# A fused attention and ELU feed-forward kernel: token blocks of 512, 512, 512 and 256 in place of four batches of 448

## The chip, the core and the metric

The kernel runs on one core of one Trainium2 chip. The metric is the device time of one execution in microseconds. Three runs of the kernel before gave 648.57, 648.53 and 648.56 us; their median is 648.56 us.

## What is computed

The reference is attention with a soft cap on the scores, followed by two dense layers with an ELU between them. All of it is float32.

```python
batch, n_heads, seq, head_dim = (4, 12, 448, 64)      # attention
n_tokens, d_model, d_ff = (1792, 768, 2048)           # layers

scores = (1 / sqrt(head_dim)) * (q @ k.T)
scores = cap * tanh(scores / cap)                     # cap = 30
attn = softmax(scores)
x = (attn @ v)  -> rows of 768 = 12 heads * 64        # 1792 tokens
h = x @ w_in
g = where(h > 0, h, exp(min(h, 0)) - 1)
out = g @ w_out
```

## The kernel before

**Numbers as pairs.** The layers' products are float32 products made of three passes. Each operand is split into a higher part and a lower part that TensorE takes in one pass each (type fp32r): `xh`, `xl` for the tokens, `wh`, `wl` for the weights, `gh`, `gl` for what comes out of the ELU. A product is `wh*xh + wh*xl + wl*xh`, three matmuls that add up in one PSUM bank. A matmul here is a pair of instructions: the weights (128 by 128) are loaded (PEld in the profile), then the columns of tokens are streamed (PE).

**Attention.** Twelve rounds, each for two of the 24 pairs of heads. The order of the work in a round is written out as a table of times (`AT`), sorted once, and each engine gets its instructions in that order. ACT does tanh and exp of the scores. VectorE (DVE) splits q and k, adds and normalises, splits the first weights, and from round 5 on also splits x of the first batch (`split`, lines 172 and 180). The table `END` orders the end of the attention, where the first hidden units start: both hidden tiles of batch 0, then the splits of batch 1.

**Layers.** `d_ff` is worked off in 8 rounds r of two hidden tiles i (FT = 2, 256 hidden channels), and in each round over the 4 batches b of 448 tokens. A unit (r, b) has a first half, `first` (lines 228 to 240): for each of two tiles, 6 channel tiles by 3 matmuls give h in PSUM, then the ELU (`elu`, lines 205 to 221) as a chain over two engines:

- ACT exp of h (line 210), DVE min and add (211), DVE max and add, reading h (214), ACT copy to `gh` (219), DVE subtract to `gl` (220).

The two hidden tiles of a unit have one PSUM bank each (`pv0`, `pv1`), so the next unit's first matmul into `pv0` waits until line 214 of the last one has read it. The second half, `second` (lines 242 to 260), gives 768 output channels as three tiles of two banks (3 buffers), which DVE adds to an accumulator in SBUF (line 268); in round 0 ACT copies instead. In the last round the accumulator is written to DRAM.

**Order.** `Moe.run` (line 273) is software pipelined by one unit: first half of unit i, three steps of a weight, second half of unit i-1, two steps of a weight. Every engine works through its own queue in that order, so an instruction that waits holds up all behind it on its engine.

**Weights.** The next round's four weight tiles come as raw 64-bit pairs and are made on the spot, in five steps (`Weights.steps`): (1) three DVE instructions, lines 107 to 109; (2) ACT, line 119; (3) DVE, line 123, then a GpSimd (POOL) add, line 126; (4) ACT copy to `wh`, line 133, which needs the POOL add; (5) DVE subtract to `wl`, line 137, which needs `wh`. With five steps a unit, each unit makes one weight, and the second half's three DVE adds stand between step 3 and step 5.

Of the kernel before, what the change touches and what calls it, by code (L numbers as in the profile page):

```python
# [7 lines left out]
F32 = mybir.dt.float32  # L8
# [9 lines left out]
P = 128  # L18
BANK = 512
# [13 lines left out]
TINY = 2.0**-15  # L33

# [30 lines left out]
class Weights:  # L65
# [4 lines left out]
    def __init__(self, nc, pool, rawp, pre, w):  # L70
        self.nc, self.pool, self.rawp, self.pre, self.w = nc, pool, rawp, pre, w
        self.late = self.now = None
        self.raw, self.split = {}, {}
        self.nraw = self.nmid = 0

    def buffer(self, k, n, width, dtype):

        if self.late and k % 2:
            tag, bufs = {"wr": ("raw", 2), "wv": ("vf", 3), "wq": ("vf", 3)}[n]
            return self.rawp.tile([P, width], dtype, name=f"{n}{k}", tag=tag, bufs=bufs)  # L80
# [3 lines left out]
        return self.pre[:, at : at + width].bitcast(dtype)  # L84

# [66 lines left out]
class Tokens:  # L152
# [6 lines left out]
    def new(self, p):  # L159
        self.x[p] = self.pool.tile([P, S], F32, name=f"x{p}", tag="x", bufs=NPAIR + 2)  # L160
        return self.x[p]

    def split(self, p):
        self.high(p)
        self.low(p)

    def high(self, p, vector=False):
        x = self.x[p]
        pool, n = (self.early, 2 * PPB) if p < 2 * PPB else (self.late, 2 * PPB)
        xh = pool.tile([P, S], F32R, name=f"xh{p}", tag="xh", bufs=n)  # L170
        if vector:
            self.nc.vector.tensor_copy(out=xh, in_=x)
        else:
            self.nc.scalar.activation(out=xh, in_=x, func=AF.Copy)
        self.parts[p] = (xh,)

    def low(self, p):
        xh = self.parts[p][0]
        xl = self.pool.tile([P, S], F32R, name=f"xl{p}", tag="x", bufs=NPAIR + 2)
        self.nc.vector.tensor_tensor(out=xl, in0=self.x.pop(p), in1=xh.bitcast(F32), op=ALU.subtract)  # L180
        self.parts[p] = (xh, xl)


class Moe:
# [15 lines left out]
    def hidden(self, r, b, i, h):  # L200
        f = r * FT + i
        for c in range(NC):
            self.products(h, self.wt.get(f, 0), c, self.x.parts[b * PPB + c], c == 0, c == NC - 1)

    def elu(self, r, b, i, h):
        nc, sb = self.nc, self.early
        f = r * FT + i
        n = f"{f}_{b}"
        ev = sb.tile([P, S], F32, name=f"e{n}", tag="ev", bufs=2)
# [7 lines left out]
        gh = sb.tile([P, S], F32R, name=f"gh{n}", tag="gh", bufs=4)  # L217
        gl = sb.tile([P, S], F32R, name=f"gl{n}", tag="gl", bufs=4)
        nc.scalar.activation(out=gh, in_=ev, func=AF.Copy)  # L219
        nc.vector.tensor_tensor(out=gl, in0=ev, in1=gh.bitcast(F32), op=ALU.subtract)  # L220
        self.g[f, b] = (gh, gl)

    def begin(self):

        t = self.ps.tile([P, 2, BANK], F32, name="h0", tag="s", bufs=3)
        return [t[:, i, :S] for i in range(FT)]

    def first(self, r, b, behind=()):

        behind = list(behind)  # L230
        for i in range(FT):
            t = self.ps.tile([P, BANK], F32, name=f"h{r * FT + i}_{b}", tag=f"pv{i}", bufs=1)
            h = t[:, :S]
            self.hidden(r, b, i, h)
            if i == 0:
                self.elu(r, b, i, h)
            for p in behind[i * 3 : i * 3 + 3]:
                self.x.split(p)
            if i:
                self.elu(r, b, i, h)  # L240

    def second(self, r, b):
        nc = self.nc
        for e in range(0, NC, 2):
            if (r, b, e) == (NR - 1, B - 1, NC - 2):
                continue
            t = self.ps.tile([P, 2, BANK], F32, name=f"o{r}_{b}_{e}", tag="s", bufs=3)
            for k in range(2):
                self.outputs(t[:, k, :S], r, b, e + k)
            if r == 0:  # L250
                o = self.late.tile([P, 2, S], F32, name=f"acc{b}_{e}", tag="acc", bufs=B * NC // 2)
                self.acc[b, e] = o
                nc.scalar.activation(out=o, in_=t[:, :, :S], func=AF.Copy)
            else:
                self.finish(r, b, e, 2, t[:, :, :S], self.acc[b, e])
        if (r, b) == (NR - 1, B - 1):
            for k in range(2):
                t = self.ps.tile([P, 1, BANK], F32, name=f"last{k}", tag=f"pv{k}", bufs=1)
                self.outputs(t[:, 0, :S], r, b, NC - 2 + k)
                self.finish(r, b, NC - 2 + k, 1, t[:, :, :S], self.acc[b, NC - 2][:, k : k + 1])  # L260

    def outputs(self, acc, r, b, e):
        for i in range(FT):
            f = r * FT + i
            self.products(acc, self.wt.get(f, 1), e, self.g[f, b], i == 0, i == FT - 1)

    def finish(self, r, b, e, n, t, o):
        self.nc.vector.tensor_tensor(out=o, in0=t, in1=o, op=ALU.add)  # L268
        if r == NR - 1:
            out = self.out[e * P : (e + n) * P, b * S : (b + 1) * S]  # L270
            self.nc.sync.dma_start(out=out.rearrange("(e p) s -> p e s", p=P), in_=o)

    def run(self):

        units = [(r, b) for r in range(NR) for b in range(B)]
        for i in range(1, len(units) + 1):
            if i < len(units):
                self.first(*units[i], range((i + 1) * PPB, min((i + 2) * PPB, NPAIR)))
            self.wt.run(WSTEPS - 2)
            self.second(*units[i - 1])  # L280
            self.wt.run(2)
            self.wt.load()


class Attention:
# [158 lines left out]
    def run(self, weights, moe, raw, rawv):  # L444
# [14 lines left out]
        for n in range(rounds):  # L459
# [55 lines left out]
def general_attention(nc, sb, ps, x, con, src, rawp):  # L515
# [62 lines left out]
def attention_elu_kernel(tc, qk, v, cap, w, out):  # L578
    nc = tc.nc
    src = (qk, v)  # L580
    with ExitStack() as outer:
        cp, rawp, xp, wp, early = (
            outer.enter_context(tc.tile_pool(name=n, bufs=1)) for n in ("con", "raw", "x", "w", "early")
# [6 lines left out]
        raw1 = cp.tile([P, QK], F32, name="raw1")  # L590
# [7 lines left out]
        def path(general):  # L598
            tag = "gf"[not general]
            with ExitStack() as ctx:  # L600
                if not general:
                    ctx.enter_context(tc.manual_schedule())
                weights = Weights(nc, wp, rawp, pre, w)
                x = Tokens(nc, xp, early)
                moe = Moe(nc, early, ps, weights, x, out)
                with tc.tile_pool(name=f"at{tag}", bufs=1) as sb, tc.tile_pool(
                    name=f"dr{tag}", bufs=1, space=DRAM
                ) as dr:
                    if general:
                        general_attention(nc, sb, ps, x, con, src, rawp)  # L610
# [3 lines left out]
                        for p in range(2 * PPB):  # L614
                            x.split(p)
# [3 lines left out]
                    else:  # L619
                        Attention(nc, sb, ps, dr, x, con, src, rawp).run(weights, moe, (raw0, raw1), rawv0)  # L620
# [54 lines left out]
```

## Time and profile before

| | before |
|---|---|
| median of three runs | 648.56 us |
| span of the profiled execution, first to last instruction | 646.2 us |
| the profiled execution in all: the profile gives no time outside its span; the median of the runs lies 2.3 us above the span | 648.6 us, if the part around the span is that of the runs |
| PE busy (records) | 633.9 us, 98% |
| weight loads (PEld) busy | 501.8 us, 78% |
| DVE busy | 462.5 us, 72% |
| ACT busy | 296.8 us, 46% |
| POOL busy | 61.4 us, 10% |
| attention, to the first matmul of the layers | 0 to 171.1 us |
| layers, to the last matmul | 171.1 to 640.7 us |

A span is counted from the first to the last instruction of the program. Ends of matmuls are modelled, so for TensorE the times from one start to the next tell more than the durations. The profile's granted TensorE clock is a share of 2.4 GHz.

### The profile page before, as it was taken

The numbers are of one execution on the slowest core, as the hardware profiler recorded it, in microseconds if no ns is written. First come the engines' busy times: TensorE is split into PE (matmuls) and PEld (weight loads), VectorE is DVE, ScalarE is ACT, GpSimd is POOL, SyncE is SP. The second block draws the span as 40 slices with busy tenths as digits, with TensorE's granted clock in tenths as the row PEclk, the third lists the DMA queues.
The fourth block names the chain that finished last, engine by engine and source line by source line (L and its number), as shares of the span: only waits on it lengthen the run. The fifth ranks groups of instructions, "written<-read, shape, count | busy, mean of one in ns | idle before, by whom it ended". The sixth has DMA issues, their size and how long they took to land.

```text
span 646.2 us, 8747 instructions
## 1 busy us (share of the span) xinstructions
PE 633.9 (98%) x3408; PEld 501.8 (78%) x3408; DVE 462.5 (72%) x672; ACT 296.8 (46%) x384; POOL 61.4 (10%) x40
## 2 busy tenths in 40 slices
PE   6999999999999999999999999999999999999996
PEld 3334434343499999999999999999999999999996
DVE  4789999999667656666677776666677776666443
ACT  6999999999816552222322222222222222222110
POOL 0010100110001121111111211111111111111000
PEclk9999999999999999999999999999999999999999
DMA  4455455543143022020202022020202022000224
GB/s 162 140 161 188 135 185 149 169 143 115 37 134 115 1 97 98 2 98 1 99 0 98 10 89 85 13 98 1 97 1 99 6 94 75 24 1 0 86 87 174
DMA packets 30064, 54.38 MB, mean 84 GB/s; under 512 B 13376, under 2 KB 19776, under 8 KB 30016
## 3 DMA queue, kind: packets, MB, share of 16 engines
q1 hardware_dynamic: 30016, 53.75, 24.8%
q8 instruction: 29, 0.48, 0.3%
q14 instruction: 19, 0.16, 0.1%
HBM read 47.97 MB, written 5.59 MB: 83 GB/s over the span
## 4 chain that ended last, share of the span: by engine, by line
PE 86%; DVE 9%; DMA 2%; issue 1%; SPq 0%; POOL 0%; DVEq 0%
PE h L196 12%; PE h L198 12%; PE h L197 12%; PE o L198 12%; PE o L197 12%; PE o L196 12%; PE pv L370 7%; PE s L328 5%; DVE u L392 3%; DVE qkl L323 2%; PE sum L401 2%; DVE num L407 1%; PE s L345 1%; DMA pre<-in_qk_dram 1%; DVE qkh L320 1%
## 5 line engine op out<-in xcount | busy, mean ns | idle before, releaser
L196 PE MATMUL h<-xh,wh 128*128 128x448 f32 x384 | 140.4, 366 | 0.0
L197 PE MATMUL h<-xl,wh 128*128 128x448 f32 x384 | 140.2, 365 | 0.0
L198 PE MATMUL h<-xh,wl 128*128 128x448 f32 x384 | 140.2, 365 | 0.0
L196 PE MATMUL o<-gh,wh 128*128 128x448 f32 x380 | 138.8, 365 | 0.0
L197 PE MATMUL o<-gl,wh 128*128 128x448 f32 x380 | 138.8, 365 | 0.0
L198 PE MATMUL o<-gh,wl 128*128 128x448 f32 x380 | 138.8, 365 | 0.0
L268 DVE TENSOR_TENSOR acc<-o,acc 128x896 f32<-128x896 f32 x83 | 85.8, 1082 | 9.4 <-PE o L198 9.4
L210 ACT ACTIVATE e<-h 128x448 f32<-128x448 f32 x64 | 34.8, 544 | 111.8 <-PE h L198 111.7
L363 ACT ACTIVATE p<-s,cap 128x896 f32<-128x896 f32 x84 | 84.8, 1009 | 2.7
L211 DVE TENSOR_SCALAR e<-e 128x448 f32<-128x448 f32 x64 | 25.1, 392 | 84.8 <-ACT e L210 84.8
L361 ACT ACTIVATE s<-s,tsc 128x896 f32<-128x896 f32 x84 | 81.9, 975 | 4.2 <-PE s L345 2.9
L370 PE MATMUL pv<-p,vf 128*64 128x448 f32 x368 | 79.3, 552 | 1.8 <-DVE num L407 1.7
L196 PEld LDWEIGHTS h<-xh,wh 128*128 128x128 f32 x384 | 72.1, 188 | 7.1 <-issue 1.4
L198 PEld LDWEIGHTS h<-xh,wl 128*128 128x128 f32 x384 | 72.1, 188 | 5.7
L197 PEld LDWEIGHTS h<-xl,wh 128*128 128x128 f32 x384 | 72.1, 188 | 5.7
L196 PEld LDWEIGHTS o<-gh,wh 128*128 128x128 f32 x380 | 71.4, 188 | 5.6
L197 PEld LDWEIGHTS o<-gl,wh 128*128 128x128 f32 x380 | 71.4, 188 | 5.6
L198 PEld LDWEIGHTS o<-gh,wl 128*128 128x128 f32 x380 | 71.4, 188 | 5.6
L219 ACT ACTIVATE gh<-e 128x448 fp32r<-128x448 f32 x64 | 37.0, 578 | 81.4 <-DVE e L214 81.4
L220 DVE TENSOR_TENSOR gl<-e,gh 128x448 fp32r<-128x448 f32 x64 | 40.0, 625 | 41.3 <-ACT gh L219 41.3
L126 POOL TENSOR_TENSOR pre<-pre,wq 128x768 int32<-128x768 int32 x18 | 34.8, 1935 | 349.0 <-DVE pre L123 349.0
L370 PEld LDWEIGHTS pv<-p,vf 128*64 128x64 f32 x368 | 22.3, 136 | 42.9 <-issue 32.0
(70 smaller groups left out, 635.8 us busy)
## 6 DMA issues: line engine op xcount, KB each, us to landing
pre<-in_w_dram SPq DMA_DIRECT2D x18, 768.0 KB, 4.2
wr<-in_w_dram SPq DMA_DIRECT2D x14, 768.0 KB, 5.6
raw<-in_qk_dram SPq DMA_DIRECT2D x22, 448.0 KB, 4.8
vf<-in_v_dram SPq DMA_DIRECT2D x23, 256.0 KB, 4.2
rb<-rec SPq DMA_DIRECT2D x48, 112.0 KB, 2.8
out_dram<-acc SPq DMA_DIRECT2D x11, 448.0 KB, 2.5
den<-sums SPq DMA_DIRECT2D x96, 1.8 KB, 2.3
out_dram<-acc SPq DMA_DIRECT2D x2, 224.0 KB, 3.2
```

The costliest lines, as they stand in the source:

```text
L126: nc.gpsimd.tensor_tensor(out=vi, in0=vi, in1=q, op=ALU.add)
L196: mm(acc, wh[:, m, :], ph, start=first, stop=False)
L197: mm(acc, wh[:, m, :], pl, start=False, stop=False)
L198: mm(acc, wl[:, m, :], ph, start=False, stop=last)
L210: nc.scalar.activation(out=ev, in_=h, func=AF.Exp)
L219: nc.scalar.activation(out=gh, in_=ev, func=AF.Copy)
L220: nc.vector.tensor_tensor(out=gl, in0=ev, in1=gh.bitcast(F32), op=ALU.subtract)
L268: self.nc.vector.tensor_tensor(out=o, in0=t, in1=o, op=ALU.add)
L328: yield lambda a=a, b=b, i=i: self.nc.tensor.matmul(s, a[o, k], b[o, :S], start=i == 0, stop=i == 2)
L361: self.nc.scalar.activation(out=s, in_=s, func=AF.Tanh, scale=self.con.tsc[:, 0:1])
L363: self.nc.scalar.activation(out=pt, in_=s, func=AF.Exp, scale=self.con.cap[:, 0:1])
L370: self.nc.tensor.matmul(out[o, :S], w[j], x[j], **flags)
```

## The change

The 1792 tokens are cut into blocks of 512, 512, 512 and 256 (`BLOCKS`), whatever the batch. A full bank of 512 columns is streamed per matmul in the first three blocks. The block of 256 holds higher and lower part side by side in one tile of 512 columns (`both`), so that `wh` takes both in one matmul of 512 columns, and `wl` takes the higher part alone in one of 256: two matmuls in place of three. Its two halves of h and of the output lie in the two halves of the bank and are added afterwards (`elu_last`, and a second add in `finish`). The split of x is done in pieces where a block crosses two batches. Weight steps go by block: 7, 7, 6 and none. The buffers of odd weights and the first loads also move to other pools. The line numbers of the changed kernel are others: line 254 to 264 there are lines 210 to 220 before, 340 is 268, 124 to 154 are 107 to 137.

```diff
+HALF = BANK // 2
+BLOCKS = [(t, min(BANK, B * S - t)) for t in range(0, B * S, BANK)]
+WRUN = (7, 7, 6, 0)
...
     def products(self, acc, w, m, part, first, last):
-        (wh, wl), (ph, pl) = w, part
-        mm(acc, wh[:, m, :], ph, start=first, stop=False)
-        mm(acc, wh[:, m, :], pl, start=False, stop=False)
-        mm(acc, wl[:, m, :], ph, start=False, stop=last)
+        (wh, wl), (ph, pl, both) = w, part
+        wh, wl = wh[:, m, :], wl[:, m, :]
+        if both is None:
+            mm(acc, wh, ph, start=first, stop=False)
+            mm(acc, wh, pl, start=False, stop=False)
+            mm(acc, wl, ph, start=False, stop=last)
+            return
+        if first:
+            mm(acc, wh, both, start=True, stop=False)
+        mm(acc[:, :HALF], wl, ph, start=False, stop=False)
+        if not first:
+            mm(acc, wh, both, start=False, stop=last)
...
+    def elu_last(self, r, t, hs):
+        two = self.ev(f"s{r}_{t}").rearrange("p (i n) -> p i n", i=FT)
+        for i, h in enumerate(hs):
+            self.nc.scalar.activation(out=two[:, i], in_=h[:, HALF:], func=AF.Copy)
+            self.nc.vector.tensor_tensor(out=two[:, i], in0=h[:, :HALF], in1=two[:, i], op=ALU.add)
+        ev = self.ev(f"{r}_{t}").rearrange("p (i n) -> p i n", i=FT)
+        self.shape(ev, two)
...
+            self.divide(ev[:, i], g[:, 0], g[:, 1])
...
+    def finish(self, r, t, e, n, s, o):
+        if r == 0:
+            self.nc.scalar.activation(out=o, in_=s[:, :, :width], func=AF.Copy)
+        else:
+            self.nc.vector.tensor_tensor(out=o, in0=s[:, :, :width], in1=o, op=ALU.add)
+        if width == HALF:
+            self.nc.vector.tensor_tensor(out=o, in0=s[:, :, HALF:], in1=o, op=ALU.add)
...
-            self.wt.run(WSTEPS - 2)
-            self.second(*units[i - 1])
-            self.wt.run(2)
-            self.wt.load()
+            n = WRUN[units[i - 1][1]]
+            self.wt.run(n // 2)
+            self.second(*units[i - 1])
+            self.wt.run(n - n // 2)
+            self.wt.ahead()
...
-                if 0 <= c < PPB:
-                    at(g + AT["split"][k], *((self.x.high, c, True) if k == 0 else (self.x.low, c)))
-        for c in range(PPB):
-            at(end + END["xh"], self.x.high, PPB + c)
-            at(end + END["xl"], self.x.low, PPB + c)
+                for p in ([c] if 0 <= c < PPB else []) + [PPB + i for i in range(PPB) if n == 8 + i // 2]:
+                    at(g + AT["split"][k], *((self.x.high, p, 0, True) if k == 0 else (self.x.low, p, 0)))
+        for b in (1, 2):
+            for c in range(PPB):
+                at(end + END["xh"], self.x.high, b * PPB + c, 1)
+                at(end + END["xl"], self.x.low, b * PPB + c, 1)
```

Three places show how the queues move. The first is TensorE's queue at the start of a unit's hidden tile (h; `xh`, `xl` or `xb` are the tokens, `wh` and `wl` the weights). Before, any batch:

```order
L196 MATMUL h_1_2058<-xh_1947,wh_522 128x448
L197 MATMUL h_1_2058<-xl_2012,wh_522 128x448
L198 MATMUL h_1_2058<-xh_1947,wl_523 128x448
L196 MATMUL h_1_2058<-xh_1949,wh_522 128x448
L197 MATMUL h_1_2058<-xl_2014,wh_522 128x448
L198 MATMUL h_1_2058<-xh_1949,wl_523 128x448
```

With the change, the block of 256 tokens:

```order
L234 MATMUL h_3_2367<-xb_2260,wh_518 128x512
L235 MATMUL h_3_2367<-xb_2260,wl_519 128x256
L235 MATMUL h_3_2367<-xb_2263,wl_519 128x256
L237 MATMUL h_3_2367<-xb_2263,wh_518 128x512
L235 MATMUL h_3_2367<-xb_2266,wl_519 128x256
L237 MATMUL h_3_2367<-xb_2266,wh_518 128x512
```

Three matmuls of 448 columns per channel tile became one of 512 and one of 256; in the other three blocks there are three of 512.

The second is DVE's queue around a unit's outputs (`acc`), with the weight steps (`pre`, `wv`, `wl`) and the ELU (`e`, `gl`). Before, in every unit:

```order
L123 SCALAR_TENSOR_TENSOR wv_2716<-wr_2552,wv_2716 128x768
L268 TENSOR_TENSOR acc_0_2292<-o_1_0_2724,acc_0_2292 128x896
L268 TENSOR_TENSOR acc_2_2307<-o_1_2_2738,acc_2_2307 128x896
L268 TENSOR_TENSOR acc_4_2322<-o_1_4_2752,acc_4_2322 128x896
L137 TENSOR_TENSOR wl_2767<-wv_2716,wh_2766 128x768
L211 TENSOR_SCALAR e_3_2791<-e_3_2791 128x448
```

With the change, from the middle of round 1 to the first ELU of round 2 (the block of 256 is `es_3`, `e_3`, `g_3`):

```order
L140 SCALAR_TENSOR_TENSOR pre<-pre 128x768
L279 TENSOR_TENSOR es_3_2813<-h_3_2787,es_3_2813 128x256
L279 TENSOR_TENSOR es_3_2813<-h_3_2800,es_3_2813 128x256
...
L154 TENSOR_TENSOR wl_2784<-pre,wh_2783 128x768
...
L340 TENSOR_TENSOR acc_4_2458<-o_2_4_2863,acc_4_2458 128x1024
L140 SCALAR_TENSOR_TENSOR wv_2829<-wr_2672,wv_2829 128x768
L154 TENSOR_TENSOR wl_2880<-wv_2829,wh_2879 128x768
L255 TENSOR_SCALAR e_0_2904<-e_0_2904 128x512
L258 SCALAR_TENSOR_TENSOR e_0_2904<-h_0_2885,e_0_2904 128x512
```

Step 3 (line 140) and step 5 (line 154) of a weight now stand next to each other, ahead of the next ELU; before, three output adds lay between them.

The third is DVE's queue in attention round 9. Before:

```order
L407 COPY num_1524<-pv_1_1472 128x448
L172 CAST xh_1528<-x_875 128x448
L320 CAST qkh_1547<-raw_1450 128x832
L323 TENSOR_TENSOR qkl_1548<-raw_1450,qkh_1547 128x832
L410 COPY sums_1562<-sum_1_1519 128x448
```

With the change:

```order
L486 COPY num_1524<-pv_1_1470 128x448
L200 CAST xh_4_1528<-x_871 128x448
L200 CAST xh_2_1207<-x_1185 128x64
L200 CAST xh_3_1366<-x_1187 128x64
L399 CAST qkh_1549<-raw_1448 128x832
```

Two small casts came in, for the 64 tokens of the second batch that belong to the first block; two small subtracts follow later in the round, and the same in rounds 8 and 10.

## Rows read from the trace of the kernel before

**Rows 1.** The page: busy tenths in 40 slices of the span, and the granted clock.

```profile
PE   6999999999999999999999999999999999999996
DVE  4789999999667656666677776666677776666443
PEclk9999999999999999999999999999999999999999
```

**Rows 2.** Busy time by stretch: PE, PEld, DVE, ACT, POOL, then PEclk, DMA share, GB/s.

```profile
92.00:157.00 65.00, 63.89 (x436) 26.26 (x436) 62.69 (x96) 63.03 (x67) 4.45 (x2) 1.00 0.51 152
330.00:388.00 58.00, 58.00 (x288) 53.76 (x287) 40.15 (x56) 15.58 (x24) 7.42 (x4) 1.00 0.15 55
```

**Rows 3.** Timeline in the layers, TensorE: start us, us, engine, line, out<-in.

```profile
300.00 0.19 PEld L198 LDWEIGHTS h<-xh,wl 128*128 128x128 f32 x1
300.20 0.36 PE L198 MATMUL h<-xh,wl 128*128 128x448 f32 x1
300.20 0.19 PEld L196 LDWEIGHTS h<-xh,wh 128*128 128x128 f32 x1
300.40 0.36 PE L196 MATMUL h<-xh,wh 128*128 128x448 f32 x1
```

**Rows 4.** Timeline of POOL, one add per unit, 20 rows from first to last.

```profile
311.62 1.85 POOL L126 TENSOR_TENSOR pre<-pre,wq 128x768 int32<-128x768 int32 x1 [12.73 <-DVE pre L123]
...
588.89 1.85 POOL L126 TENSOR_TENSOR wv<-wv,wq 128x768 int32<-128x768 int32 x1 [12.75 <-DVE wv L123]
```

**Rows 5.** Timeline of the weight loads in attention, four rows from first to last.

```profile
150.40 0.14 PEld L370 LDWEIGHTS pv<-p,vf 128*64 128x64 f32 x2 [0.23 <-issue]
...
151.52 0.14 PEld L370 LDWEIGHTS pv<-p,vf 128*64 128x64 f32 x2 [0.23 <-issue]
```

**Rows 6.** Timeline of one unit of the layers, DVE, ACT and POOL.

```profile
335.29 0.39 DVE L211 TENSOR_SCALAR e<-e 128x448 f32<-128x448 f32 x1 [1.32 <-ACT e L210]
335.71 0.62 DVE L214 SCALAR_TENSOR_TENSOR e<-h,e 128x448 f32<-128x448 f32 x1
336.37 0.58 ACT L219 ACTIVATE gh<-e 128x448 fp32r<-128x448 f32 x1 [1.12 <-DVE e L214]
...
336.98 0.63 DVE L220 TENSOR_TENSOR gl<-e,gh 128x448 fp32r<-128x448 f32 x1 [0.65 <-ACT gh L219]
337.53 0.95 DVE L107 SCALAR_TENSOR_TENSOR pre<-pre 128x768 f32<-128x768 f32 x1
...
339.70 0.96 DVE L123 SCALAR_TENSOR_TENSOR pre<-pre 128x768 int32<-128x768 int32 x1
340.57 3.08 DVE L268 TENSOR_TENSOR acc<-o,acc 128x896 f32<-128x896 f32 x3
...
340.80 1.86 POOL L126 TENSOR_TENSOR pre<-pre,wq 128x768 int32<-128x768 int32 x1 [12.72 <-DVE pre L123]
...
342.69 0.85 ACT L133 ACTIVATE wh<-pre 128x768 fp32r<-128x768 f32 x1 [4.93 <-POOL pre L126]
343.57 0.96 DVE L137 TENSOR_TENSOR wl<-pre,wh 128x768 fp32r<-128x768 f32 x1
```

**Rows 7.** Groups by shape: line 268, count, busy us, mean ns, idle before.

```profile
L268 DVE TENSOR_TENSOR acc<-o,acc 128x896 f32<-128x896 f32 x83 | 85.8, 1082 | 9.4 <-PE o L198 9.4
...
L268 DVE TENSOR_TENSOR acc<-last,acc 128x448 f32<-128x448 f32 x2 | 1.2, 624 | 0.7 <-PE last L198 0.6
```

**Rows 8.** Timeline of DVE: a cast in attention, and the splits at its end.

```profile
149.84 0.38 DVE L172 CAST xh<-x 128x448 fp32r<-128x448 f32 x1
150.14 0.58 DVE L320 CAST qkh<-raw 128x832 fp32r<-128x832 f32 x1
...
178.93 3.29 DVE L180 TENSOR_TENSOR xl<-x,xh 128x448 fp32r<-128x448 f32 x6
```

**Rows 9.** Timeline at the end of the span: the last output add.

```profile
641.08 0.62 DVE L268 TENSOR_TENSOR acc<-last,acc 128x448 f32<-128x448 f32 x1 [0.60 <-PE last L198]
```

**Rows 10.** Timeline of POOL: one of its four adds in attention.

```profile
143.74 2.64 POOL L126 TENSOR_TENSOR pre<-pre,wq 128x768 int32<-128x768 int32 x1 [27.90 <-DVE pre L123]
```

More of the change, by code (lines that the diff above doesn't have):

```diff
@@ L33, with pieces @@
 TINY = 2.0**-15
+HALF = BANK // 2
+BLOCKS = [(t, min(BANK, B * S - t)) for t in range(0, B * S, BANK)]
+NB = len(BLOCKS)
+WRUN = (7, 7, 6, 0)
+def pieces(b):
+    out = []
+    for t, (t0, n) in enumerate(BLOCKS):
+        lo, hi = max(t0, b * S), min(t0 + n, (b + 1) * S)
+        if lo < hi:
+            out.append((t, lo - t0, lo - b * S, hi - lo))
+    return out
 K0 = D
@@ L84, in buffer, with ahead @@
         return self.pre[:, at : at + width].bitcast(dtype)
+    def ahead(self):
+        self.load(self.nmid + 2 - self.nraw)
     def load(self, n=1):
@@ L159, in new, with split, piece, high @@
     def new(self, p):
-        self.x[p] = self.pool.tile([P, S], F32, name=f"x{p}", tag="x", bufs=NPAIR + 2)
+        self.x[p] = self.pool.tile([P, BANK], F32, name=f"x{p}", tag="x", bufs=NPAIR + 1)[:, :S]
         return self.x[p]
[L163 to L170, printed above, removed]
+    def split(self, p, t):
+        self.high(p, t)
+        self.low(p, t)
+    def piece(self, p, t):
+        return next((o, at, n) for k, o, at, n in pieces(p // PPB) if k == t)
+    def high(self, p, t, vector=False):
+        c = p % PPB
+        o, at, n = self.piece(p, t)
+        if (t, c) not in self.parts:
+            if t == NB - 1:
+                both = self.late.tile([P, 2, HALF], F32R, name=f"xb{c}", tag="xb", bufs=PPB)
+                self.parts[t, c] = [both[:, 0], both[:, 1], both.rearrange("p a n -> p (a n)")]
+            else:
+                pool, k = (self.early, 2 * PPB) if t < 2 else (self.late, PPB)
+                xh = pool.tile([P, BANK], F32R, name=f"xh{t}_{c}", tag="xh", bufs=k)
+                self.parts[t, c] = [xh, None, None]
+        out, x = self.parts[t, c][0][:, o : o + n], self.x[p][:, at : at + n]
         if vector:
-            self.nc.vector.tensor_copy(out=xh, in_=x)
+            self.nc.vector.tensor_copy(out=out, in_=x)
         else:
[L174 to L181, printed above, removed]
+            self.nc.scalar.activation(out=out, in_=x, func=AF.Copy)
+    def low(self, p, t):
+        c = p % PPB
+        o, at, n = self.piece(p, t)
+        part = self.parts[t, c]
+        if part[1] is None:
+            part[1] = self.pool.tile([P, BANK], F32R, name=f"xl{t}_{c}", tag="x", bufs=NPAIR + 1)
+        h, l = (a[:, o : o + n] for a in part[:2])
+        self.nc.vector.tensor_tensor(out=l, in0=self.x[p][:, at : at + n], in1=h.bitcast(F32), op=ALU.subtract)
 class Moe:
@@ L216, in elu, with divide @@
         )
[L217 to L221, printed above, removed]
+    def divide(self, ev, gh, gl):
+        self.nc.scalar.activation(out=gh, in_=ev, func=AF.Copy)
+        self.nc.vector.tensor_tensor(out=gl, in0=ev, in1=gh.bitcast(F32), op=ALU.subtract)
@@ new lines, in elu @@
+    def elu(self, r, t, i, h):
+        f = r * FT + i
+        ev = self.ev(f"{f}_{t}")
+        self.shape(ev, h)
+        gh, gl = self.parts(f"{f}_{t}")
+        self.divide(ev, gh, gl)
+        self.g[f, t] = (gh, gl, None)
+    def elu_last(self, r, t, hs):
[5 more added lines that the diff above has]
+        self.shape(ev, two)
+        for i in range(FT):
+            f = r * FT + i
+            g = self.early.tile([P, 2, HALF], F32R, name=f"g{f}_{t}", tag=("gh", "gl")[i], bufs=4)
+            self.divide(ev[:, i], g[:, 0], g[:, 1])
+            self.g[f, t] = (g[:, 0], g[:, 1], g.rearrange("p a n -> p (a n)"))
@@ L223, in begin, with first @@
     def begin(self):
         t = self.ps.tile([P, 2, BANK], F32, name="h0", tag="s", bufs=3)
-        return [t[:, i, :S] for i in range(FT)]
-    def first(self, r, b, behind=()):
-        behind = list(behind)
+        return [t[:, i] for i in range(FT)]
+    def first(self, r, t, behind=()):
+        hs = []
         for i in range(FT):
[L232 to L240, printed above, removed]
@@ L242, in second @@
-    def second(self, r, b):
+            h = self.ps.tile([P, BANK], F32, name=f"h{r * FT + i}_{t}", tag=f"pv{i}", bufs=1)
+            hs.append(h)
+            self.hidden(r, t, i, h)
+            if t < NB - 1 and i == 0:
+                self.elu(r, t, i, h)
+            for p, k in behind:
+                if p % PPB // 3 == i:
+                    self.x.split(p, k)
+            if t < NB - 1 and i:
+                self.elu(r, t, i, h)
+        if t == NB - 1:
+            self.elu_last(r, t, hs)
@@ L243, in second @@
+    def second(self, r, t):
         nc = self.nc
+        end = (r, t) == (NR - 1, NB - 1)
         for e in range(0, NC, 2):
-            if (r, b, e) == (NR - 1, B - 1, NC - 2):
+            if end and e == NC - 2:
                 continue
-            t = self.ps.tile([P, 2, BANK], F32, name=f"o{r}_{b}_{e}", tag="s", bufs=3)
+            s = self.ps.tile([P, 2, BANK], F32, name=f"o{r}_{t}_{e}", tag="s", bufs=3)
             for k in range(2):
-                self.outputs(t[:, k, :S], r, b, e + k)
+                self.outputs(s[:, k], r, t, e + k)
@@ L250, in second @@
             if r == 0:
[L251 to L256, printed above, removed]
+                self.acc[t, e] = self.late.tile(
+                    [P, 2, BLOCKS[t][1]], F32, name=f"acc{t}_{e}", tag=f"acc{t}", bufs=NC // 2
+                )
@@ L257, in second @@
+            self.finish(r, t, e, 2, s, self.acc[t, e])
+        if end:
             for k in range(2):
[L258 to L262, printed above, removed]
+                s = self.ps.tile([P, 1, BANK], F32, name=f"last{k}", tag=f"pv{k}", bufs=1)
+                self.outputs(s[:, 0], r, t, NC - 2 + k)
+                self.finish(r, t, NC - 2 + k, 1, s, self.acc[t, NC - 2][:, k : k + 1])
@@ L269, in finish @@
         if r == NR - 1:
[L270 removed]
+            out = self.out[e * P : (e + n) * P, t0 : t0 + width]
             self.nc.sync.dma_start(out=out.rearrange("(e p) s -> p e s", p=P), in_=o)
     def run(self):
[L275 removed]
+        units = [(r, t) for r in range(NR) for t in range(NB)]
         for i in range(1, len(units) + 1):
             if i < len(units):
[L278 to L279 removed]
+                behind = ()
+                if i + 1 < NB:
+                    behind = [(b * PPB + c, i + 1) for c in range(PPB) for b in range(B)
+                              if any(k == i + 1 for k, *_ in pieces(b))]
+                self.first(*units[i], behind)
+            n = WRUN[units[i - 1][1]]
+            self.wt.run(n // 2)
```

68 lines of the change are left out of this document (36 added, 32 removed).

## The prediction

> **What bounds the kernel now.** I read the page's slices first, then the busy time of two stretches, then single instructions.
>
> TensorE is busy in every slice and its clock is granted in full [rows 1], so 2.4 GHz. In the layers PE is busy without a gap, the weight loads for 53.8 of 58 us, DVE for 40 [rows 2]. A busy PE is not yet one that streams all the time: 448 columns at 2.4 GHz are 186.7 ns, but one POOL add per unit gives a unit of 277.27 / 19 = 14.593 us, and a unit has 72 matmuls: 202.7 ns each [rows 4]. Where the other 16 ns go is seen in the timeline [rows 3]: the load of the next weights starts when the last matmul starts, takes 0.19, and the next matmul starts at its end. The period is that of the load, not of the stream. A load of 64 columns in attention takes 0.14, and there two float32 passes of 448 columns repeat every 1.12 / 3 = 0.373 us, 186.7 per pass, with 0.23 of idle time ahead of the next load [rows 5]: where the load is short, the stream sets the period and adds next to nothing. So in the layers I take the period as the longer of (columns / 2.4 GHz) and 202.7 ns.
>
> In the attention from 92 to 157 us it is DVE that is full, 62.7 of 65 us, and PE waits now and then [rows 2].
>
> **The sum for TensorE.** Before: 2304 matmuls of 202.7 ns, 467.0 us. The columns in all stay the same: per weight tile 4 x 3 x 448 = 5376 before, and 9 x 512 + 512 + 256 = 5376 after. What changes is how many loads there are and what hides them. Of 512 columns there are 192 x 10 = 1920. Their stream is 213.3 ns, longer than the load, so the load is covered; rounding of [rows 5] leaves up to 1.6 ns on top and I take 215. Bounds: 213.3, and 229.3 if the 16 ns come on top of any stream. Of 256 columns there are 192; their stream of 106.7 ns cannot cover the load, so 202.7 (bounds 122.7 and 202.7). Sum 412.8 + 38.9 = 451.7: **15.3 us less**, if nothing makes TensorE wait.
>
> The Trainium skill (TensorE: Matmul & The Clock Gate, "Back-to-back issue gap" and "LDWEIGHTS") gives N / 2.4 + 2.5 ns per matmul and P / 1.2 = 107 ns for a load of 128 columns. By it no load would be seen before, a matmul of 448 would take 189 ns, and the change would save only the 2.5 ns of 192 matmuls, 0.5 us. The trace differs: 202.7 [rows 4], and a load of 0.19 us [rows 3].
>
> **DVE's queue in the layers.** DVE waits for ACT, so for TensorE's h, 1.3 us ahead of an ELU [rows 6]: it has slack. The new order takes it. A round now has 240 x 215 + 24 x 202.7 ns = 56.5 us of TensorE. DVE's round, from start to start:
>
> - an ELU of 448 columns takes 2.24 (335.29 to 337.53, [rows 6]). 64 columns more add 0.03 in line 211 and some 0.06 in each of the three others (line 268: 458 ns for 448 columns, 1.02 a column, [rows 7]): 2.47. Six of them: 14.8;
> - an output add of 896 repeats every 1.00 [rows 6], of 1024 every 1.13. Nine: 10.2;
> - a weight takes 337.53 to 340.57 = 3.04, and line 137 0.88 before the next can follow: 3.92. Four: 15.7;
> - the block of 256: two adds of halves, the ELU of both tiles as one, two subtracts of 256, with its waits for ACT, 3.8; six output adds of 512, the second of each pair after the first, 4.0;
> - waits that were covered. Line 137 starts 2.92 after line 123 has ended (340.66 to 343.57, [rows 6]), for the add on POOL and the copy on ACT; three output adds fill this now. With 7, 7 and 6 steps in one queue, step 5 stands right behind step 3 twice in a round, ahead of block 1's outputs and of the next round's first ELU. Nothing lies between: 2 x 2.9. A third time DVE's next instruction is the block of 256's first add, which waits for an ACT copy that is queued behind the same `wh`: 3.2. Together 9.0.
>
> That makes 57.6 us, **1.1 more than TensorE's round**. Who waits: the first bank of h is free again only when the ELU's line 214 has read it, and in front of that ELU stands step 5 of the round's last weight; so TensorE waits at the start of block 1 of the next round. Round 0 adds its outputs on ACT, round 7 makes no weights; rounds 1 to 6 remain: 6 x 1.1 = 6.6 us. Bounds: 0, if the real round is 1.1 shorter, and 6 x 3.5 if POOL is slow (below).
>
> **Attention.** From 92 to 157 us each DVE instruction more is on the path. New are 12 casts and subtracts of 64 columns in rounds 8 to 10. A cast of 448 repeats after 0.30 [rows 8], so 0.10 with 64; a subtract after 3.29 / 6 = 0.54, so 0.14. Six casts and four subtracts fall before PE takes over: 0.6 + 0.5 = 1.1 us. The last two subtracts come where DVE has gaps. Bounds: 0.8 by columns alone, 2.0 with whole durations.
>
> **Transition.** Six splits of 448 took 3.29 us [rows 8]. Now there are six of 384 (0.47) and then six of 128 (0.20), and the first channel tile of block 1 needs one of each: it is ready 2.8 + 0.2 after the start, not 0.6. TensorE comes to it with the two hidden tiles of 512 some 0.5 earlier: +0.5 (0 to 1). The splits for block 2 take 0.7 longer, under a second half of 7.7 us: nothing.
>
> **End.** The last add is 0.62 [rows 9]; now there are two of 256, 0.43 each: +0.2. The transfers behind it get smaller; I take nothing off. The moved buffers cost nothing: the first transfers have the same sizes and order, and an odd weight's load, which now waits for attention to end, is needed a unit later.
>
> **Sum.** -15.3 + 6.6 + 1.1 + 0.5 + 0.2 = -6.9. The profiled execution spans 646.2 us, 2.3 under the median of the runs; with that part unchanged it would be 639.3 in the span and **641.7 us** in the median.
>
> **Rivals.**
>
> *DVE's queue keeps its cover* (chance 0.22). My round is 57.6 against 56.5, 2% apart, and four of its terms are scaled to sizes that the trace does not have. If it is 56.5 or less, TensorE never waits: -15.3 + 1.8 = -13.5, 635.1 us.
>
> *The 16 ns are a cost of every matmul* (0.08), not of the load: 1920 x 229.3 + 192 x 122.7 = 463.8, 3.2 less; TensorE's round is then 58.0, longer than DVE's: 647.2 us, no difference that counts. The load that starts with the last matmul and ends with the next speaks against it [rows 3], and so does attention [rows 5]. The same page of the Trainium skill has such a fixed cost per matmul, 2.5 ns. By it the change is worth 0.5 us, so slower by 1.3 with the rest.
>
> *The POOL add is slower in its new place* (0.12), which ends **slower than before**. It took 1.85 in the layers but 2.64 in attention [rows 10], where DVE's adds from SBUF ran at the same time. Three times in a round DVE waits for it directly. At 2.64 each wait is 0.8 longer, DVE's round is 60.0, TensorE waits 3.5 in six rounds: -15.3 + 21 + 1.8 = +7.5, 656.1 us. It decides from a DVE round of 58.7 on (12.9 us of gain left, over 6 rounds, 2.2 each). Against it: DVE stands still during two of these adds.
>
> *Both floors hold* (0.06): 512 columns at 229.3 and 256 at 202.7 make 479.1 us, +12.1 + 1.8: 662.5. It decides above 222 ns for a matmul of 512.
>
> That the change does not do what it says is excluded: the order of TensorE's queue shows the 512s and 256s.
>
> **How the numbers follow.** 641.7 is the likeliest (0.52), with 638 to 646 as its own range: a DVE round from 57.0 to 58.2 and the small terms. The range for 8 in 10 takes in the two rivals next to it, 635.1 and 647.2: 634.5 to 648. What stays out is the slow POOL add and the two floors, 0.18. A measurement of this kernel can tell 0.2%, 1.3 us, from no change. Faster by more: the forecast, the first rival and a little of the second, 0.76. Within: 0.09. Slower: 0.15.
>
> **What would show it.** Right: matmuls of 512 starting 215 ns apart and the one behind a 256 after 203; TensorE without a gap except about 1 us at the start of block 1 in rounds 2 to 7, ended by line 258 on DVE; DVE waits of 2.9 ahead of line 154 twice a round, and 3.2 ahead of line 279; the first hidden matmul at 172.2 us. Wrong: 512s at 229 ns, or no wait at block 1, or waits of several us per round, or attention longer by more than 2 us.

## The result, and the profile after

The changed kernel takes 653.74 us (median of 4 runs, 653.09 to 653.96), the kernel before 648.55 beside it: a ratio of 1.0081, 95% interval 1.0067 to 1.0095. It is **slower by 5.2 us**, where 6.9 less was forecast. The profiled execution took 653.74 us with a span of 651.9.

The page of the changed kernel: engine totals and the slices that answer to [rows 1].

```profile
PE 628.7 (96%) x3216; PEld 451.7 (69%) x3216; DVE 480.1 (74%) x721; ACT 298.2 (46%) x404; POOL 61.1 (9%) x40
...
PE   6999999999999899999999999999999999999996
...
PEclk9999999999999899999999999999999999999999
```

Slice 14 is new: PE has an 8 there, and so has the granted clock. Two stretches of the changed kernel show it in numbers; the second answers to [rows 2]. Columns: stretch and length, busy time of PE, PEld, DVE, ACT, POOL, then the granted clock, DMA share and GB/s.

```profile
204.00:262.00 58.00, 55.27 (x249) 45.76 (x248) 35.90 (x58) 26.08 (x43) 8.66 (x5) 0.97 0.18 57
330.00:388.00 58.00, 57.19 (x264) 47.43 (x263) 42.04 (x59) 15.40 (x25) 7.38 (x4) 1.00 0.17 55
```

In the layers TensorE now waits: once 2.7 us, and six times 0.8, besides 0.3 at the start of the layers' second unit. The list of waits in the changed kernel tells for what (total, times, longest, us):

```profile
DVE wl L154 <- ACT wh L150: 43.8, 15, 2.9
...
DVE es L279 <- ACT es L278: 25.1, 9, 3.2
...
PE h L228 <- DVE e L258: 4.8, 6, 0.8
...
PE o L228 <- ACT acc L338: 2.7, 1, 2.7
```

**The matmuls.** The timeline of TensorE in the changed kernel, ahead in a block of 512 and behind in the block of 256 (start, length, engine, line, out<-in); it answers to [rows 3].

```profile
307.70 0.39 PE L228 MATMUL h<-xh,wh 128*128 128x512 f32 x1
...
308.83 0.39 PE L230 MATMUL h<-xh,wl 128*128 128x512 f32 x1
...
340.10 0.27 PE L235 MATMUL h<-xb,wl 128*128 128x256 f32 x1
340.21 0.40 PE L237 MATMUL h<-xb,wh 128*128 128x512 f32 x1
340.45 0.28 PE L235 MATMUL h<-xb,wl 128*128 128x256 f32 x1
340.56 0.39 PE L237 MATMUL h<-xb,wh 128*128 128x512 f32 x1
```

From 307.70 to 308.83 five matmuls start, one every 226 ns (the median of all in the big blocks is 227). In the block of 256 the pair repeats after 0.35 us: 0.115 from the 256 to the 512, 0.235 from the 512 to the 256. The loads of the same stretch:

```profile
340.11 0.19 PEld L237 LDWEIGHTS h<-xb,wh 128*128 128x128 f32 x1
340.22 0.19 PEld L235 LDWEIGHTS h<-xb,wl 128*128 128x128 f32 x1
```

Two loads start 0.11 apart and each is drawn 0.19 long. So 0.19 is how long one load takes to get through, not how often one can be had: it bounds nothing here.

**The wait at block 1**, as it stands in rounds 2 to 7, here at the start of round 4. Timeline of the changed kernel, DVE and TensorE, and DVE on to the next round's wait:

```profile
360.54 0.96 DVE L154 TENSOR_TENSOR wl<-wv,wh 128x768 fp32r<-128x768 f32 x1 [2.92 <-ACT wh L150]
361.41 0.40 PE L237 MATMUL o<-g,wh 128*128 128x512 f32 x1
361.87 0.69 DVE L258 SCALAR_TENSOR_TENSOR e<-h,e 128x512 f32<-128x512 f32 x1
362.62 0.50 PE L228 MATMUL h<-xh,wh 128*128 128x512 f32 x1 [0.81 <-DVE e L258]
362.96 0.40 PE L229 MATMUL h<-xl,wh 128*128 128x512 f32 x1
...
388.16 0.43 DVE L255 TENSOR_SCALAR e<-e 128x512 f32<-128x512 f32 x1 [1.05 <-ACT e L254]
...
394.50 0.96 DVE L154 TENSOR_TENSOR wl<-wv,wh 128x768 fp32r<-128x768 f32 x1 [2.92 <-ACT wh L150]
...
405.07 0.76 DVE L279 TENSOR_TENSOR es<-h,es 128x256 f32<-128x256 f32 x2 [3.17 <-ACT es L278]
...
419.03 0.96 DVE L154 TENSOR_TENSOR wl<-wv,wh 128x768 fp32r<-128x768 f32 x1 [2.92 <-ACT wh L150]
419.90 0.42 DVE L255 TENSOR_SCALAR e<-e 128x512 f32<-128x512 f32 x1
```

From 361.41 to 362.62 are 1.21 us where a 512 takes 0.23, and the next start comes 0.11 late: 1.09 us, six times, 6.5. A round lasts from 361.42 to 419.90 in DVE's rows, 58.5 us.

**Round 0.** The same kernel's timeline of DVE, POOL, ACT and TensorE around slice 14:

```profile
218.84 0.95 DVE L140 SCALAR_TENSOR_TENSOR wv<-wr,wv 128x768 int32<-128x768 int32 x1
220.01 1.82 POOL L143 TENSOR_TENSOR wv<-wv,wq 128x768 int32<-128x768 int32 x1 [11.94 <-DVE wv L140]
220.55 0.40 PE L237 MATMUL h<-xb,wh 128*128 128x512 f32 x1
221.86 0.84 ACT L150 ACTIVATE wh<-wv 128x768 fp32r<-128x768 f32 x1 [3.67 <-POOL wv L143]
222.61 1.01 ACT L338 ACTIVATE acc<-o 128x1024 f32<-128x1024 f32 x1
223.67 0.79 PE L228 MATMUL o<-gh,wh 128*128 128x512 f32 x1 [2.73 <-ACT acc L338]
224.26 0.63 PE L229 MATMUL o<-gl,wh 128*128 128x512 f32 x1
...
226.82 0.53 PE L229 MATMUL o<-gl,wh 128*128 128x512 f32 x1
227.19 0.39 PE L230 MATMUL o<-gh,wl 128*128 128x512 f32 x1
```

Block 2's first output needs a PSUM tile that still holds block 1's. In round 0 ACT empties it (line 338), but ACT's queue has step 4 of weight 5 in front (`wh`, line 150), which waits for POOL, and POOL for DVE's step 3. TensorE stands from 220.55 to 223.67, 2.9 us more than its matmul, and the granted clock then falls: 224.26 to 226.82 are 6 starts of 427 ns, which is 512 columns at 1.2 GHz. From 223.67 to 227.19 eight matmuls take 3.52 us where 8 x 0.227 = 1.8 were due. So the place costs 2.9 + 1.7 = **4.6 us**.

**Account.** TensorE: a round has 216 matmuls of 227.0 ns and 24 pairs of 350, 57.4 us, 459.5 in all, against 467.0 before: -7.5. Block 1: +6.5. Round 0: +4.6. The three places that close it are three lines of the timeline, for the start of the layers, for the wait in the transition, and for the end:

```profile
172.31 0.50 PE L228 MATMUL h<-xh,wh 128*128 128x512 f32 x1
...
184.03 0.50 PE L229 MATMUL h<-xl,wh 128*128 128x512 f32 x1 [0.27 <-DVE xl L211]
...
647.22 0.42 DVE L342 TENSOR_TENSOR acc<-last,acc 128x256 f32<-128x256 f32 x1
```

The layers start 1.2 later (171.10 before). The second matmul of block 1 starts 0.66 behind the one ahead of it, 0.43 more than its period, and the next comes 0.1 late: +0.5. At the end four adds of 256 now follow each other behind the last matmul, which starts at 645.61; the last of them ends at 647.64, 2.0 later, where it was 641.70 behind 640.68, 1.0 [rows 9]. The span ends 6.3 behind that matmul's start, against 5.5: +0.8. Sum -7.5 + 6.5 + 4.6 + 1.2 + 0.5 + 0.8 = +6.1; the spans differ by 651.9 - 646.2 = 5.7. The 0.4 lies in the first term, which goes by medians: with the means of the same starts, 226.9 ns and 349 for a pair, TensorE's sum is 459.1, 7.9 less than before. The medians of the runs differ by 5.2: the profiled execution takes 1.8 us more than its span now, and the median before lay 2.3 above the span.

### The profile page after: what moved, and what is told of

Its sections match the earlier page's. It is cut to its first block, busy times and chain, and to the rows that moved or that the text cites. A ratio compares the mean times of both kernels' runs of the same rounds, so it can differ in the third digit from the quotient of the medians.

```text
span 651.9 us, 8444 instructions
## 1 busy us (share of the span) xinstructions
PE 628.7 (96%) x3216; PEld 451.7 (69%) x3216; DVE 480.1 (74%) x721; ACT 298.2 (46%) x404; POOL 61.1 (9%) x40
## 4 chain that ended last, share of the span: by engine, by line
PE 43%; DVE 33%; ACT 7%; POOL 6%; DMA 6%; issue 3%; SPq 1%; POOLq 0%; DVEq 0%; ACTq 0%
PE h L228 7%; DVE acc L340 7%; PE h L229 6%; PE h L230 6%; PE pv L449 4%; PE o L228 4%; PE o L229 4%; PE o L230 4%; POOL wv L143 4%; DVE wl L154 3%; DVE u L471 3%; PE s L407 3%; DVE e L258 3%; ACT wh L150 2%; POOL pre L143 2%
## 5 line engine op out<-in xcount | busy, mean ns | idle before, releaser
L228 PE MATMUL h<-xh,wh 128*128 128x512 f32 x288 | 113.0, 392 | 4.8 <-DVE e L258 4.8
L228 PE MATMUL o<-gh,wh 128*128 128x512 f32 x288 | 112.9, 392 | 2.7 <-ACT acc L338 2.7
L229 PE MATMUL o<-gl,wh 128*128 128x512 f32 x288 | 112.6, 391 | 0.0
L229 PE MATMUL h<-xl,wh 128*128 128x512 f32 x288 | 112.3, 390 | 0.3 <-DVE xl L211 0.3
L230 PE MATMUL o<-gh,wl 128*128 128x512 f32 x288 | 112.5, 391 | 0.0
L230 PE MATMUL h<-xh,wl 128*128 128x512 f32 x288 | 112.0, 389 | 0.0
L340 DVE TENSOR_TENSOR acc<-o,acc 128x1024 f32<-128x1024 f32 (+1 forms) x83 | 87.3, 1088 | 6.3 <-PE o L230 6.1
L263 ACT ACTIVATE gh<-e 128x512 fp32r<-128x512 f32 x48 | 30.3, 632 | 89.2 <-DVE e L258 89.2
L230 PEld LDWEIGHTS o<-gh,wl 128*128 128x128 f32 x288 | 54.5, 189 | 11.5
L229 PEld LDWEIGHTS o<-gl,wh 128*128 128x128 f32 x288 | 54.5, 189 | 11.4
L230 PEld LDWEIGHTS h<-xh,wl 128*128 128x128 f32 x288 | 54.1, 188 | 11.4
L264 DVE TENSOR_TENSOR gl<-e,gh 128x512 fp32r<-128x512 f32 x48 | 33.3, 693 | 33.5 <-ACT gh L263 33.5
L254 ACT ACTIVATE e<-h 128x512 f32<-128x512 f32 x48 | 28.3, 591 | 46.5 <-PE h L230 46.5
```

What stands on the lines that cost most here:

```text
L228: mm(acc, wh, ph, start=first, stop=False)
L229: mm(acc, wh, pl, start=False, stop=False)
L230: mm(acc, wl, ph, start=False, stop=last)
L263: self.nc.scalar.activation(out=gh, in_=ev, func=AF.Copy)
L264: self.nc.vector.tensor_tensor(out=gl, in0=ev, in1=gh.bitcast(F32), op=ALU.subtract)
L340: self.nc.vector.tensor_tensor(out=o, in0=s[:, :, :width], in1=o, op=ALU.add)
```

## The experiments

The theory after the result: TensorE gains 7.5 us by having fewer matmuls, and loses 11 us to the order of the weight steps, at two places that are independent of each other. The rivals: the added adds of the block of 256 fill DVE in any order; the load of the weights is a floor after all.

**Five steps per unit, everywhere.** The blocks and matmuls are as changed; the weight steps go back to the order before.

```diff
-            n = WRUN[units[i - 1][1]]
-            self.wt.run(n // 2)
+            self.wt.run(3)
             self.second(*units[i - 1])
-            self.wt.run(n - n // 2)
+            self.wt.run(2)
```

> The changed kernel with one whole weight (5 steps) per unit, 3 steps ahead of the second half and 2 behind it, as in the kernel before; blocks and matmuls as changed. Theory (queue): the 7, 7, 6 split alone makes TensorE wait, 6.5 us at the start of block 1 in rounds 2 to 7 and 4.6 us in round 0 (wait for an output bank, then half clock). Both go: 653.7 - 11.1 = 642.6 us, no wait of TensorE over 0.5 us in the layers. Rival (DVE is full by the added work of the block of 256, in any order): the waits move to another block, and the time stays within 2 us of 653.7.

Measured: 642.31 us (641.66 to 642.73), 0.9907 of the kernel before (0.9892 to 0.9922). The two stretches of this kernel:

```profile
204.00:262.00 58.00, 58.00 (x269) 48.38 (x268) 38.42 (x60) 26.84 (x44) 9.24 (x5) 1.00 0.21 69
330.00:388.00 58.00, 58.00 (x269) 48.38 (x268) 43.39 (x61) 15.89 (x25) 8.05 (x5) 1.00 0.18 57
```

PE is full in both and the clock too, with more DVE work per us than in the changed kernel (43.39 against 42.04). DVE was not full; its queue stood in the wrong order. The list of waits of this kernel for the same instructions:

```profile
DVE e L254 <- ACT e L253: 55.1, 37, 3.5
...
DVE wl L153 <- ACT wh L149: 9.9, 4, 3.0
```

The waits for `wh` fall from 43.8 us to 9.9, and DVE now waits for TensorE's h by way of ACT's exp (24.2 us in the changed kernel, 55.1 here): the slack that [rows 6] showed is back. This kernel beats both others. It has the moved buffers too, which no run takes back alone. The terms without them, -7.5 for TensorE, +0.9 for the start of the layers (172.02), +0.5 and +0.2 for the end, make -5.9; the kernel before took 648.43 us beside it, 6.1 more. So the buffers cost nothing that can be seen here.

**The two places apart.** Five steps per unit ("fives") in round 0 alone; in the second kernel `> 0` stands for `== 0`, fives in the later rounds alone.

```diff
             n = WRUN[units[i - 1][1]]
-            self.wt.run(n // 2)
+            k = n // 2
+            if units[i - 1][0] == 0:
+                n, k = WSTEPS, 3
+            self.wt.run(k)
             self.second(*units[i - 1])
-            self.wt.run(n - n // 2)
+            self.wt.run(n - k)
```

> Changed kernel, 5 steps per unit in round 0 alone, 7, 7, 6, 0 in the other rounds. Theory: the wait for an output bank in round 0 and the half clock behind it go, the six waits at block 1 stay: 653.7 - 4.6 = 649.1 us. Rival (round 0 is only late because DVE comes late out of attention): no change, 653.7.

> Changed kernel, 7, 7, 6, 0 steps in round 0 alone, 5 per unit in the rounds after it. Theory: round 0 keeps its 4.6 us, the six waits at block 1 of 1.1 us go: 653.7 - 6.5 = 647.2 us. Rival (DVE full in any order): within 1 us of 653.7. Together with the kernel with fives in round 0 alone: the two differences must add up to that with fives everywhere.

Measured: 649.20 us (11 runs, 648.73 to 649.60) and 646.76 (11 runs, 645.29 to 648.44). The differences to 653.74 are 4.5 and 7.0, together 11.5; with both 11.4. So the terms add up, and the first is as large as the rows of round 0 made it, within 0.1. The second kernel's runs lie 3.2 us apart, so its 7.0 and the expected 6.5 cannot be told from each other. The stretches of the kernel with fives in round 0 alone:

```profile
204.00:262.00 58.00, 58.00 (x269) 48.39 (x268) 40.72 (x64) 28.03 (x45) 9.23 (x5) 1.00 0.20 69
330.00:388.00 58.00, 57.18 (x263) 47.47 (x262) 42.37 (x59) 15.56 (x25) 6.90 (x5) 1.00 0.16 54
```

Round 0 is healed with its clock, the later wait is untouched, and the layers start as late as in the changed kernel (172.33 and 172.31): so lateness out of attention alone does not make the wait. ACT's timeline in this kernel shows what does; block 1's outputs are copied ahead of `wh` now, where they stood behind it before:

```profile
217.15 2.85 ACT L338 ACTIVATE acc<-o 128x1024 f32<-128x1024 f32 x3
222.33 0.85 ACT L150 ACTIVATE wh<-wv 128x768 fp32r<-128x768 f32 x1 [2.33 <-POOL wv L143]
```

In the other kernel the list of waits keeps only the first of the two:

```profile
PE o L228 <- ACT acc L338: 2.6, 1, 2.6
```

**The block of 256 without the merge.** Three plain matmuls of 256 columns, and no second adds; the steps stay 7, 7, 6, 0.

```diff
-        if first:
-            mm(acc, wh, both, start=True, stop=False)
-        mm(acc[:, :HALF], wl, ph, start=False, stop=False)
-        if not first:
-            mm(acc, wh, both, start=False, stop=last)
+        acc = acc[:, : ph.shape[-1]]
+        mm(acc, wh, ph, start=first, stop=False)
+        mm(acc, wh, pl, start=False, stop=False)
+        mm(acc, wl, ph, start=False, stop=last)
...
-            self.nc.vector.tensor_tensor(out=o, in0=s[:, :, HALF:], in1=o, op=ALU.add)
```

> Changed kernel with the block of 256 not merged: three matmuls of 256 columns per weight tile instead of one of 512 and one of 256, a plain ELU per hidden tile, no second output adds; steps 7, 7, 6, 0 kept. Theory (every matmul costs columns / 2.4 GHz and some 10 ns, the load of the weights is no floor): a weight tile takes 3 x 0.115 = 0.345 us instead of 0.350, so TensorE loses nothing (-1 us in all), DVE loses 3 to 4 us of work per round and the waits at block 1 go (-6.5), the wait in round 0 stays: about 646 us. Rival (a weight load of 0.19 us is a floor for a row of narrow matmuls, the single 256 between two 512s was spared it): 3 x 0.19 to 0.20 = 0.57 to 0.61 us per weight tile, 192 tiles: +42 to +50 us, with the waits gone 690 to 697 us.

Measured: 648.98 us (11 runs, 647.26 to 649.32), 4.8 less than the changed kernel, where 8 less was expected. TensorE's timeline in this kernel:

```profile
337.88 0.28 PE L229 MATMUL h<-xb,wh 128*128 128x256 f32 x1
...
339.08 0.28 PE L230 MATMUL h<-xb,wh 128*128 128x256 f32 x1
```

Ten starts, 0.12 us each: no floor of 0.19. But three of them are 0.360, not 0.345, against 0.350 for the pair: the merge saves 10 ns in each of 192 pairs, 1.9 us, which the expectation had taken for nothing. TensorE's wait at block 1 is gone with the DVE work that was left out, though the order of the steps is the same; only its second matmul still comes 0.11 late there (361.49 to 361.83). The wait in round 0 stays (2.5 us). -6.5 + 1.9 = -4.6 is close to the 4.8, but two terms stand beside it: +0.7 for six such late matmuls, and -1.2 at the end, where the span ends 5.1 us behind the last matmul's start, against 6.3. Together -5.1, so 0.3 stays open.

**Both at once**, fives and no merge, the first and the last of these edits together:

> Changed kernel with both: one whole weight per unit (3 steps ahead, 2 behind) and the block of 256 in three plain matmuls of 256. If three matmuls of 256 cost TensorE no more than the pair of 512 and 256, the time is that of the kernel with fives alone or up to 1.5 us less: 641 to 642.5 us. Rival (the single 256 in a pair is cheap only between 512s; a row of 256s is slower): over 643.5 us.

Measured: 643.59 us (5 runs, 643.50 to 643.72), 1.3 above the kernel with fives alone. That is just on the rival's side: a row of 256s is slower than the pair, though by the 10 ns shown above and not by a floor. With the order mended the merge is worth its 1.9 us on TensorE, less 0.7 at the end, where the span ends 5.1 us behind the last matmul's start here and 5.8 with the merge.

**What a matmul costs.** Two kernels, profiled once each, whose widths go down from round to round.

```diff
+WIDTH = (512, 448, 384, 320, 256, 192, 128, 64)
+COLS = 128
...
-            mm(acc, wh, pl, start=False, stop=False)
-            mm(acc, wl, ph, start=False, stop=last)
+            for _ in range(BANK // n):
+                mm(acc[q, :n], wh[:, q], pl[:, :n], start=False, stop=False)
+                if _ < BANK // n - 1:
+                    mm(acc[q, :n], wl[:, q], ph[:, :n], start=False, stop=False)
+            mm(acc[i, :n], wl[:, i], ph[:, :n], start=False, stop=last)
```

(`n` is the round's width; `q` is `COLS` columns of the weights, `i` too but for the last of an accumulation.)

> Changed kernel in which the matmuls of the three big blocks, but for the first of each accumulation, take 512, 448, 384, 320, 256, 192, 128 and 64 columns in rounds 0 to 7, and are repeated 1, 1, 1, 1, 2, 2, 4 and 8 times so that TensorE stays the busy engine (the outputs leave out the columns that are not taken). Read: the time from start to start in each round. Theory (a cost of every matmul): columns / 2.4 GHz plus 8 to 16 ns at each width down to 64: 227, 202.7, 175, 148, 117, 91, 64, 38 ns. Rival A (a load of 128 columns is a floor): flat at some width, 0.19 if the recorded duration of the load counts. Rival B (a floor of its own for fp32r matmuls below some width): a step upward as the width falls.

> The same with 64 columns of the weights in place of 128 in all matmuls but the first and last of an accumulation (half of the output rows leave out their products). If the 13.7 to 16 ns on top of columns / 2.4 GHz belong to the load of the weights, they fall with half of the columns to load: 448 columns in 187 to 195 ns instead of 202.7. If they belong to the matmul, every width takes the same as with 128 columns, within 2 ns.

Two widths of TensorE's timeline with 128 columns of the weights, the first and the last of a row of starts each:

```profile
232.15 0.36 PE L236 MATMUL h<-xl,wh 128*128 128x448 f32 x1
...
232.96 0.36 PE L239 MATMUL h<-xh,wl 128*128 128x448 f32 x1
...
516.14 0.28 PE L238 MATMUL h<-xh,wl 128*128 128x128 f32 x1
...
516.81 0.27 PE L239 MATMUL h<-xh,wl 128*128 128x128 f32 x1
```

and with 64 columns of the weights:

```profile
233.83 0.36 PE L236 MATMUL h<-xl,wh 128*64 128x448 f32 x1
...
234.64 0.37 PE L239 MATMUL h<-xh,wl 128*64 128x448 f32 x1
...
579.82 0.22 PE L236 MATMUL h<-xl,wh 128*64 128x64 f32 x1
...
580.34 0.22 PE L238 MATMUL h<-xh,wl 128*64 128x64 f32 x1
```

448 columns: 0.81 / 4 = 202 ns in both kernels. 128 columns at 128 weight columns: 0.67 / 6 = 112; 64 at 64 weight columns: 0.52 / 9 = 58. The medians of all such starts at the full clock:

| columns | / 2.4 GHz | 128 weight columns | 64 weight columns |
|---|---|---|---|
| 512 | 213 | 227 | 227 |
| 448 | 187 | 205 | 202 |
| 384 | 160 | 174 | 173 |
| 320 | 133 | 147 | 145 |
| 256 | 107 | 120 | 113 |
| 192 | 80 | 111 | 89 |
| 128 | 53 | 111 | 60 |
| 64 | 27 | 112 | 58 |

Both the theory and rival A are half right. From 320 columns up a matmul costs its columns and 12 to 18 ns, and half of the weight columns change that by 3 ns at most. Below, a load is a floor, but it is 111 ns for 128 weight columns and 58 for 64, far from the recorded 0.19 and 0.14. With 64 weight columns, 128 to 256 columns have only 6 to 9 ns on top: it is not one constant, and no run tells what it consists of. No step upward was seen as the width falls (rival B). The theory had 38 ns for 64 columns, without a floor. (In most of the first kernel's last round the granted clock fell to half, and the period rose to 213 ns. That round took 264 us, where it took 86 with 64 weight columns; this is most of what lies between their 878 and 676 us.)

The Trainium skill (TensorE: Matmul & The Clock Gate, "LDWEIGHTS") gives P / 1.2 ns for a load of P columns, by estimate 107 for 128 and 53 for 64; the floors of 111 and 58 agree with that within 5 ns. The same page of the Trainium skill ("Back-to-back issue gap") has 2.5 ns on top of a matmul's columns as the gap of a single matmul; in this row of loads and matmuls 12 to 18 were measured from 320 columns up.

## Why the prediction was wrong

- **The step that failed first: "The period is that of the load, not of the stream."** [Rows 3] show a load that begins with one matmul and is drawn until the next. That was read as cause; it is a load that has time to spare. The 16 ns at 448 come with every matmul: with half of the weight columns to load it takes 202 ns and not 205. So 512 columns cost 227.0 and not 215, and a 256 next to a 512 some 115 and not 202.7. TensorE's sum is -7.5, not -15.3. This alone moves the forecast from 641.7 to 649.5, out of the range; round 0 alone, below, would have left it at 646.3, inside. The rival "a cost of every matmul" had the mechanism, at 0.08; it overcharged (16 ns on all, 463.8 us against 459.5), because at 512 the cost is 13.7: 1728 x 2.3 ns is 4.0 of the 4.3. The other evidence for the load, [rows 5], is of float32 passes on half of the array's columns; no run here tells why they repeat with nothing on top.
- **The step that was missing: round 0.** The prediction left it out of DVE's queue because "Round 0 adds its outputs on ACT". ACT's queue has the same weight steps in it. (DVE's queue "in every unit" before the change, as it stands ahead of the prediction, is that of rounds 1 to 6: in round 0 ACT copies instead of the three adds, and round 7 has no weight steps.) The prediction counted what stands behind `wh` on ACT once, for the block of 256 (3.2 us, found: 3.17), and not for the output copies; a fall of the granted clock is in none of its terms. 2.9 us of wait and 1.7 of half clock make 4.6, and the kernel with fives in round 0 alone is 4.5 faster.
- **Right in place, and in size by luck: the wait at block 1**, 6.5 us against 6.6, in rounds 2 to 7, released by line 258, with DVE's waits of 2.92 ahead of line 154 and 3.17 ahead of line 279. But the reason was not quite the one given. "57.6 us, 1.1 more than TensorE's round" compared two closed rounds (its terms add up to 57.5). In the rows above DVE itself waits 1.05 at 388.16 for TensorE's h; its own round is 58.5 - 1.05 = 57.4, no longer than TensorE's 57.4. The loop runs through both: TensorE from 362.62 to block 2's h, then DVE from 388.16 to line 258 of the next round. That second stretch is what the uncovered waits make too long. A TensorE round 0.9 longer than forecast was therefore no relief; by the prediction's own rule it would have left 57.6 - 57.4 = 0.2 a round, 1.2 us in all. Taking DVE work out of that stretch (no merge, all but 0.11 a round) or the uncovered waits (fives) removes it.
- **Right: attention** 1.2 (1.1), **transition** 0.5 (0.5). POOL was not slower in its new place: 1.82 to 1.86 us. (In that rival 13.5 us of gain were left, not 12.9; it still decides from 58.7 on.)
- **Too small: the end**, 0.8 and not 0.2. Four adds queue there; the prediction counted what the last two take more.
- **What the sum gives with these mended**: 639.3 in the span, + 7.8 + 4.6 + 0.6 = 652.3; measured 651.9. The range failed because -15.3 stood under the forecast and under two of the rivals, 0.86 of the chance, on one reading of a recorded duration at the one width that the trace had in its layers.

The blocks and the merge by themselves are a gain: 642.31 us with the old order of steps, where the kernel before takes 648.43.

## What to carry to other kernels

The length that the profile draws for a weight load says how long it takes to get through, not the rate: look for two loads that start closer together before calling it the bound. When steps are regrouped in one program order, walk every engine's queue, in every phase where an engine has another job: a step that waits on a chain of three engines blocks whatever stands behind it on each of them. And two engines that both have slack over a round can still wait for each other, if one round's loop runs through part of each.

## What the runs showed of the hardware

- Matmuls of these layers follow each other 12 to 18 ns later than their columns at 2.4 GHz need, from 320 to 512 columns, with 64 weight columns at most 3 ns less than with 128. At the half clock nothing is on top: 512 columns in 427 ns, 384 in 320 and 320 in 267, which is columns / 1.2 GHz.
- A load of 128 weight columns can follow another after 111 ns, of 64 after 58, while the profile draws them 0.19 and 0.14 us long. At the half clock the 64-column matmuls with 128 weight columns repeat after 213 ns: that floor goes with the clock.
- One wait of 2.9 us in a TensorE that had been busy was followed by the granted half clock, in which eight matmuls took 1.7 us more. That is over half as much again as the wait itself, and no list of waits shows it; the granted clock does. It does not always follow: in the kernel of the widths with 128 weight columns the same wait, at the same place and as long, left the clock at 1.00, with the matmuls behind it 0.23 us apart. A line of TensorE's timeline there, and the row of the stretch around it:

```profile
223.63 0.50 PE L234 MATMUL o<-gh,wh 128*128 128x512 f32 x1 [2.93 <-ACT acc L347]
...
172.00:230.00 58.00, 54.80 (x250) 43.23 (x249) 37.65 (x76) 27.09 (x57) 5.49 (x3) 1.00 0.28 83
```
